# Scan and gated FFN on one core: the scan of chunks 1 to 5 as one unit of four batches, with B and C loaded as rows and turned on VectorE

## The chip, the core and the metric

The kernel runs on one core of a Trainium2 chip. A core has five engines with a queue each: TensorE (PE; its weight loads are shown as PEld), VectorE (DVE), ScalarE (ACT), GpSimd (POOL) and SyncE (SP), which here only issues DMAs. The metric is the device time of one execution in microseconds (us); of several runs the median is given.

## What is computed

A chunked state-space scan with 4 batches of 8 heads, 768 tokens, head size 32 and state size 16, and behind it a gated FFN over all 3072 tokens (model size 256, inner size 1536). Everything is float32.

```python
for c in range(nc):                                  # scan, per batch and head
    cum = np.cumsum(np.log(a)[chunk]); L = exp(cum[:, None] - cum[None, :]) * causal
    y_intra = ((C @ B.T) * L) @ x                    # within the chunk
    y_inter = (C @ state) * exp(cum)                 # from the state before
    state = exp(sum) * state + sum_j B_j x_j exp(cum[-1] - cum_j)
x = y.transpose(0, 2, 1, 3).reshape(B * S, H * D)    # then the FFN
out = (sigmoid(x @ w_gate) * (x @ w_val)) @ w_out
```

## The kernel before

**Chunks.** The 768 tokens are cut into six chunks of 128, each as two halves of 64. For each chunk the scan gives 4 x 128 = 512 rows of x, and the FFN runs over these 512 rows: twelve slices f of the inner size, each with a gate product `pg` and a value product `pv` (`products_of`, L784, six matmuls each, in which both operands are split into a high and a low part, `xh`/`xl` and `w`), then four output blocks `po` (`proj`, L821, L822, and L810 for chunk 0). I call the FFN over a chunk's rows its pass. In the pass of chunk 0 the first six slices take the weights whole (L775, the thin part), and the weights still arrive: each is clipped and split in five steps on VectorE, ScalarE and GpSimd (`split_w`, L323 to L336) and later cut into two parts (`part_w`, L351, L353).

**The scan before.** Chunk 0 has a class of its own (`FirstUnit`). For chunks 1 to 5 a unit is one chunk of one batch, and two batches share a step on TensorE. For each unit `products` turns B and C of 128 tokens on TensorE (`nc.tensor.transpose`, L393, L394, into the tile `pt`), and ScalarE copies and masks them (L404, L408, tile `bct`). For each pair there is then a product C times B (`multiply`, L473, 16 matmuls; I call it the multiply), on VectorE its weighing by the decays (`weigh`, L487), then on TensorE the product with x and with the decayed B (`within`, L499 and L506, 48 matmuls; 40 in the last chunk), on VectorE two masked local states (`chosen`, L514; L541), and on TensorE the part from the state before (L550, 16 matmuls; I call it the inter). ScalarE and VectorE cut the result into `xh` and `xl` (L564, L570). The decays come from a scan on VectorE of 128x512 for each unit (L428), whose rows `ab` are broadcast by DMA from a DRAM tile `a_z` that the kernel has written itself; the products of decays `pp` come in the same way from `a_p`.

**What sets the order.** `run()` is a planner in the kernel's own code: it takes the steps (`step(engine, cost, needs, makes)`) in the order of due times (the table `DUES` and rules such as `AHEAD`, `UNIT_T`, `STATE`) and of its own estimates, and writes one fixed instruction order for each engine. Each engine then runs its list in that order and waits at an instruction for what it needs. SP issues all loads and stores in one queue with eight lanes: a DMA waits until the DMA eight places before it is complete. PSUM gives three banks in turn (`ps_mm`) to `pg`, `pv` and `po`, so each such product needs the bank that was used three products before, and that is freed by ScalarE's sigmoid (for `pg`) or VectorE's multiplication (for `pv`, L735 in chunk 0, L739 later).

Of the kernel before, what the change touches and what calls it, by code (L numbers as in the profile page):

```python
# [8 lines left out]
F32 = mybir.dt.float32  # L9
# [37 lines left out]
GV0 = 1.75  # L47
# [22 lines left out]
def tile_ssd_then_gated_ffn(  # L70
# [25 lines left out]
    NDEC = 6  # L96
    NPRE = 5
# [163 lines left out]
    c4 = Cm.rearrange("b h s n -> s (b h) n")  # L261
    got = {}

    def pair_of(tag, c, b, shape):

        k = tag, c, b // 2
        if k not in got:
# [756 lines left out]
```

## Time and profile before

| what | value |
|---|---|
| three runs | 376.8, 377.87 and 378.27 us, median 377.87 us |
| the profiled execution | span 375.7 us from the first to the last instruction (no other time is given for it) |
| TensorE busy | 365.3 us, 97% |
| VectorE, ScalarE, GpSimd busy | 155.8, 151.2 and 153.9 us (41%, 40%, 41%) |
| first `pg` of chunk 0 | 24.70 us |
| first `pg` of chunk 1 | 98.03 us |
| first `pg` of chunk 5 | 322.68 us |
| end of the last `po` | 372.40 us |
| mean granted TensorE clock | 0.995 |

A busy share is an average over the whole span; what a change in one stage is worth is read from the timeline of that stage. The name left of an arrow in a row is what is written, the names right of it are read, x is the count. For float32 matmuls of the scan, and for L810, the trace has two records for each instruction. A bracket [0.67 <- ...] in a timeline row is idle time ahead of it and what ended it.

### The profile page before, as it was taken

How to read it: one execution, taken by the hardware profiler on the slowest of the kernel's cores; microseconds unless marked ns; L12 is line 12 of the kernel's file. 1: busy time of each engine (PE TensorE's matmuls, PEld its weight loads, DVE VectorE, ACT ScalarE, POOL GpSimd, SP SyncE). 2: the span in 40 equal slices, each digit the busy share in tenths (PEclk: the TensorE clock that was granted, in tenths of full speed). 3: DMA queues.
4: the chain of work that ended last, by engine and by line, in shares of the span. 5: the costliest groups of instructions: out<-in, count | busy, mean ns of one | idle time of the engine just before them, and what ended most of it. 6: DMA issues, size and time to landing. Idle time of an engine off the chain costs nothing.

```text
span 375.7 us, 8098 instructions
## 1 busy us (share of the span) xinstructions
PE 365.3 (97%) x3360; PEld 286.3 (76%) x3360; DVE 155.8 (41%) x280; ACT 151.2 (40%) x319; POOL 153.9 (41%) x161
## 2 busy tenths in 40 slices
PE   8879999989999999999999999999999999999996
PEld 2565478758788888887788888788877788888885
DVE  4774755854874234253431452550132440122201
ACT  2567578223536421436510435420335420244400
POOL 4346557573669540245430055430145420145410
PEclk9999999989999999999999999999999999999999
DMA  7998964087520043415502303120000000000000
GB/s 153 139 352 181 226 241 155 30 126 142 107 50 16 0 88 69 67 49 58 91 9 58 97 4 39 34 38 30 28 3 2 2 2 28 30 0 0 2 28 28
DMA packets 89270, 26.27 MB, mean 70 GB/s; under 512 B 76306, under 2 KB 82002, under 8 KB 89234
## 3 DMA queue, kind: packets, MB, share of 16 engines
q1 hardware_dynamic: 89234, 25.76, 30.7%
q8 instruction: 26, 0.43, 0.5%
q14 instruction: 10, 0.08, 0.1%
HBM read 22.41 MB, written 3.34 MB: 69 GB/s over the span
## 4 chain that ended last, share of the span: by engine, by line
PE 78%; SPq 12%; DMA 7%; issue 1%; DVE 1%; POOL 0%; DVEq 0%; POOLq 0%
PE pg L784 22%; PE pv L784 22%; PE po L821 15%; PE po L822 7%; SPq L275 4%; PE po L810 4%; DMA wr<-in_moe_w_gate_dram 3%; SPq L313 2%; PE pcb L499 2%; DMA a_z<-a 2%; SPq L309 2%; SPq L282 2%; SPq L288 2%; PE pcb L473 2%; DMA cn<-in_C_dram 2%; PE pcb L550 1%
## 5 line engine op out<-in xcount | busy, mean ns | idle before, releaser
L745 POOL TENSOR_TENSOR h<-g,h 128x512 fp32r<-128x512 f32 x60 | 79.0, 1316 | 124.6 <-ACT h L743 122.0
L784 PE MATMUL pg<-xh,w 128*128 128x512 f32 x264 | 93.8, 396 | 0.0
L784 PE MATMUL pv<-xh,w 128*128 128x512 f32 x264 | 93.7, 396 | 0.0
L821 PE MATMUL po<-w,h 128*128 128x512 f32 x228 | 81.8, 402 | 0.0
L739 DVE TENSOR_TENSOR g<-pv,g 128x512 f32<-128x512 f32 x60 | 41.4, 691 | 91.4 <-PE pv L784 86.6
L743 ACT CAST h<-g 128x512 fp32r<-128x512 f32 x60 | 37.3, 621 | 78.4 <-DVE g L739 78.4
L822 PE MATMUL po<-w,h 128*128 128x256 f32 x228 | 63.9, 280 | 0.0
L784 PEld LDWEIGHTS pg<-xh,w 128*128 128x128 f32 x264 | 49.5, 188 | 11.4 <-issue 0.5
L784 PEld LDWEIGHTS pv<-xh,w 128*128 128x128 f32 x264 | 49.6, 188 | 10.6 <-issue 0.2
L784 PE MATMUL pg<-xl,w 128*128 128x512 f32 x132 | 51.5, 390 | 0.0
L784 PE MATMUL pv<-xl,w 128*128 128x512 f32 x132 | 51.4, 390 | 0.0
L821 PEld LDWEIGHTS po<-w,h 128*128 128x128 f32 x228 | 42.8, 188 | 10.7 <-issue 0.2
L715 ACT ACTIVATE g<-pg 128x512 f32<-128x512 f32 x72 | 43.1, 599 | 19.4 <-PE pg L784 13.7
L822 PEld LDWEIGHTS po<-w,h 128*128 128x128 f32 x228 | 43.0, 189 | 0.2
L837 ACT COPY o<-po 128x256 f32<-128x256 f32 x20 | 7.5, 373 | 67.3 <-PE po L822 66.7
L839 DVE TENSOR_TENSOR o<-po,o 128x256 f32<-128x256 f32 x20 | 8.5, 425 | 59.8 <-ACT o L837 59.7
L353 POOL TENSOR_TENSOR w<-wr,w 128x512 fp32r<-128x512 f32 x18 | 24.7, 1371 | 14.2 <-ACT w L351 10.8
L428 DVE TENSOR_TENSOR_SCAN ab<-ab,delta 128x512 f32<-128x512 f32 x20 | 26.5, 1331 | 5.6 <-DMA ab<-a_z 5.6
L784 PEld LDWEIGHTS pv<-xl,w 128*128 128x128 f32 x132 | 24.8, 188 | 4.7
L784 PEld LDWEIGHTS pg<-xl,w 128*128 128x128 f32 x132 | 24.8, 188 | 4.6
L810 PE MATMUL po<-wr,h 128*128 128x256 f32 x96 | 24.9, 409 | 0.0
L336 POOL TENSOR_TENSOR wr<-wr 128x512 int32<-128x512 int32 x18 | 21.6, 1207 | 6.3 <-ACT wr L334 3.7
(106 smaller groups left out, 377.4 us busy)
## 6 DMA issues: line engine op xcount, KB each, us to landing
ab<-a_z SPq DMA_DIRECT2D x40, 128.0 KB
wr<-in_moe_w_gate_dram SPq DMA_DIRECT2D x6, 512.0 KB
wr<-in_moe_w_val_dram SPq DMA_DIRECT2D x6, 512.0 KB
wr<-in_moe_w_out_dram SPq DMA_DIRECT2D x6, 512.0 KB
out_dram<-o SPq DMA_DIRECT2D x24, 128.0 KB
xn<-in_x_dram SPq DMA_DIRECT2D x10, 256.0 KB
bn<-in_B_dram SPq DMA_DIRECT2D x10, 128.0 KB
cn<-in_C_dram SPq DMA_DIRECT2D x10, 128.0 KB
```

Source lines behind the costliest of these rows:

```text
L275: nc.sync.dma_start(t[:, b % 2 : b % 2 + n].rearrange("p b h n -> p (b h) n"), src[cs, b * H : (b + n) * H])
L336: nc.gpsimd.tensor_tensor(out=lw.bitcast(I32), in0=hw.bitcast(I32), in1=lw.bitcast(I32), op=ALU.add)
L353: engines[eng].tensor_tensor(out=lo, in0=lw, in1=hi.bitcast(F32), op=ALU.subtract)
L428: nc.vector.tensor_tensor_scan(out=t.rearrange("p h l -> p (h l)"), data0=t.rearrange("p h l -> p (h l)"), data1=delta.rearrange("p h l -> ...
L715: nc.scalar.activation(gs[k, f], pm, AF.Sigmoid)
L739: nc.vector.tensor_tensor(out=g, in0=pm, in1=g, op=ALU.mult)
L743: copies[eng](hh, g)
L745: engines[eng].tensor_tensor(out=hl, in0=g, in1=hh.bitcast(F32), op=ALU.subtract)
L784: nc.tensor.matmul(pm, w[:, part, kt, fs], xx[:, kt], start=(i == 0), stop=(i == 3 * NK - 1))
L810: nc.tensor.matmul(acc[:, :DM], hs[k, f][:, js], whole[NF + f // 2][:, f % 2], start=start, stop=stop, skip_group_check=True,)
L821: nc.tensor.matmul(acc, hh, w.rearrange("p i m -> p (i m)"), start=start, stop=False, skip_group_check=True)
L822: nc.tensor.matmul(acc[:, :DM], hl, w[:, 0, :], start=False, stop=stop, skip_group_check=True)
```

## The change

Chunk 0 keeps its units by batch. For chunks 1 to 5 the class `Scan` takes all four batches at once: one multiply of 32 matmuls (L505), four weighings in place (L509), one `within` of 96 matmuls (L520, L527; 80 in the last chunk), one `chosen` and one addition of 128x256, one inter of 32 matmuls (L469), one pair of `xh`, `xl` halves of 128x512.

B and C are no longer turned on TensorE. `load_rows` loads them in another arrangement (`bq`, `cq`): a partition is a head and one of 32 groups of four tokens, and holds 4 x 16 values in a row, 256 bytes. Each of B and C comes in eight loads per chunk, one for each batch and group of heads. VectorE then turns each batch by one transpose instruction in blocks of 32x32 (`turned`, L387), and ScalarE masks the turned C for all four batches in two instructions of 128x512 (`masked`, L400). B is still loaded a second time as tokens (`bn`) for the decayed B.

```diff
-            nc.tensor.transpose(pt[:, :L], bn, eye)
-            nc.tensor.transpose(pt[:, L : 2 * L], cn, eye)
-            yield step("act", 0.9 if c else 1.1, [], [("bct", u)], **{hold: -1})
+                for b in range(NB):
+                    nc.vector.transpose(
+                        t[:, b].rearrange("p (t f) -> p f t", f=NQ),
+                        got[tag, c][:, b].rearrange("p g (f n) -> p f g n", f=NQ),
+                    )
...
+        rows = src[:, :, c * L : (c + 1) * L].rearrange("b (q g) (t f) n -> b g q t (f n)", g=NG, f=NQ)
+        return [lambda b=b, g=g: nc.sync.dma_start(t[:, b, g], rows[b, g]) for b in range(NB) for g in range(NG)]
...
+            for b in range(NB):
+                multiply(pcb[:, :, b * L : (b + 1) * L], self.bt[:, b], self.cg[:, b])
+            for b in range(NB):
+                yield step("dve", 0.7, [("cb", c), ("scan", c, b), ("bdec", c)], [("mult", c)])
+                dec = got["ab", c]
+                weigh(dec[:, b], pcb[:, :, b * L : (b + 1) * L], dec[:, b])
```

Other loads are joined too: `ab` comes in two loads per chunk instead of eight, `bn` and `xn` in one each. Fading the state moves to GpSimd (`faded`, L426), as does the addition of the next state (L497). The table `DUES` is new, so the plan is new on every engine; one line of it before and after:

```diff
-    "result5_1": 271.1, "decays5_3": 170.5, "value4_1": 242.8, "value4_6": 193.7, "value4_7": 305.22, "value4_8": 307.96,
+    "p2_1": -0.1, "bq2_3": -64.1, "result0_0": 17.3,
```

TensorE, in the pass of chunk 4, where the scan of chunk 5 stands between the FFN's products. Before (`pt` are the turned B and C, `pcb20` the bank of the pair):

```order
L784 MATMUL pv4_6_3291<-xh4_2819,w7_569 128x512
L393 MATMUL pt5_3_3301<-eye_88,bn5_1_2678 128x128
L394 MATMUL pt5_3_3301<-eye_88,cn5_1_2680 128x128
L784 MATMUL pg4_7_3304<-xh4_2819,w6_553 128x512
L784 MATMUL pg4_7_3304<-xl4_2820,w6_553 128x512
L784 MATMUL pg4_7_3304<-xh4_2819,w6_553 128x512 x2
L784 MATMUL pg4_7_3304<-xl4_2820,w6_553 128x512
L784 MATMUL pg4_7_3304<-xh4_2819,w6_553 128x512
L499 MATMUL pcb20_3181<-m5_0_3208,xn5_0_2767 32x64 x16
L506 MATMUL pcb20_3181<-xn5_0_2767,bd5_0_2775 32x64 x4
L499 MATMUL pcb20_3181<-m5_1_3210,xn5_0_2767 32x64 x16
L506 MATMUL pcb20_3181<-xn5_0_2767,bd5_1_2779 32x64 x4
```

After, at the same pass (`bt`, `cg` are the turned B and the turned and masked C of all four batches):

```order
L793 MATMUL pv4_9_3117<-xh4_2705,w9_650 128x512
L520 MATMUL pcb5_3058<-ab5_2898,xn5_3006 32x64 x16
L527 MATMUL pcb5_3058<-xn5_3006,bd5_3091 32x64 x4
L520 MATMUL pcb5_3058<-ab5_2898,xn5_3006 32x64 x16
L527 MATMUL pcb5_3058<-xn5_3006,bd5_3091 32x64 x4
L520 MATMUL pcb5_3058<-ab5_2898,xn5_3006 32x64 x16
L527 MATMUL pcb5_3058<-xn5_3006,bd5_3091 32x64 x4
L520 MATMUL pcb5_3058<-ab5_2898,xn5_3006 32x64 x16
L527 MATMUL pcb5_3058<-xn5_3006,bd5_3091 32x64 x4
L793 MATMUL pg4_10_3214<-xh4_2705,w10_693 128x512
```

The four turns are gone, and three blocks stand where ten pieces stood: the multiply behind `pg8`, the `within` behind `pv9`, the inter behind `pv10`, with three and two products between them. (In the pass of chunk 1 the blocks stand behind `pg11` and among the first `po`.)

SP, loads for chunk 1 while chunk 0 is in its pass. Before:

```order
L313 DMA wr14_503<-in_moe_w_out_dram 128x2x512
L275 DMA bn1_0_523<-in_B_dram 128x16x16
L275 DMA cn1_0_525<-in_C_dram 128x16x16
L313 DMA wr16_540<-in_moe_w_out_dram 128x2x512
L309 DMA wr11_550<-in_moe_w_val_dram 128x2x512
L313 DMA wr13_560<-in_moe_w_out_dram 128x2x512
L313 DMA wr15_567<-in_moe_w_out_dram 128x2x512
L895 DMA a_z_109<-a0_113 32x12x64
L898 DMA a_p_110<-a1_114 32x768
L288 DMA ab2_0_701<-a_z_109 64x512 x2
```

After:

```order
L281 DMA cq1_377<-in_C_dram 128x1x64 x3
L275 DMA xn1_571<-in_x_dram 128x32x32
L293 DMA pp1_576<-a_p_110 128x1x128 x4
L305 DMA wr11_592<-in_moe_w_val_dram 128x2x512
L281 DMA bq1_331<-in_B_dram 128x1x64
L287 DMA ab1_600<-a_z_109 64x2048
L281 DMA cq1_377<-in_C_dram 128x1x64 x2
L309 DMA wr15_639<-in_moe_w_out_dram 128x2x512
L287 DMA ab1_600<-a_z_109 64x2048
L281 DMA cq1_377<-in_C_dram 128x1x64
```

`a_z` and `a_p` now go out ahead of two of the weights, and the last of the sixteen row loads of B and C is the last load ahead of the first stores.

VectorE, the same time, the end of chunk 0's pass. Before (`h0_8` frees the bank of `pv` of slice 8):

```order
L323 TENSOR_SCALAR wr15_567<-wr15_567 128x512
L735 TENSOR_TENSOR h0_8_755<-pv0_8_725,g0_8_732 128x512
L428 SCALAR_TENSOR_TENSOR ab2_0_701<-ab2_0_701,delta_99 128x512
L735 TENSOR_TENSOR h0_9_789<-pv0_9_765,g0_9_776 128x512
L330 TENSOR_SCALAR wr14_503<-wt14_757 128x512
```

After:

```order
L319 TENSOR_SCALAR wr15_639<-wr15_639 128x512
L387 STREAM_TRANSPOSE ct1_705<-cq1_377 128x4x32 x4
L744 TENSOR_TENSOR h0_8_711<-pv0_8_685,g0_8_682 128x512
L326 TENSOR_SCALAR wr13_468<-wt13_714 128x512
L408 SCALAR_TENSOR_TENSOR ab1_600<-ab1_600,delta_99 128x512
```

The four transposes of C stand ahead of `h0_8`, so the bank of `pv` of slice 8 comes free only behind the last row load of C.

## Rows read from the trace of the kernel before

**Rows 1.** The page's part on the engines: busy us, share of the span, instructions.

```profile
PE 365.3 (97%) x3360; PEld 286.3 (76%) x3360; DVE 155.8 (41%) x280; ACT 151.2 (40%) x319; POOL 153.9 (41%) x161
```

**Rows 2.** The waits of TensorE over the whole span: who waited for whom, us in total, times, longest.

```profile
PE pt L394 <- DMA cn<-in_C_dram: 2.4, 2, 1.7
...
PE pcb L506 <- POOL bd L438: 0.7, 1, 0.7
...
PE pt L393 <- DMA bn<-in_B_dram: 0.2, 1, 0.2
```

**Rows 3.** The timeline of TensorE, the pass of chunk 5, in which no scan is left: its first product, its first `po`, and its last block (start, length).

```profile
322.68 0.40 PE L784 MATMUL pg<-xh,w 128*128 128x512 f32 x1
...
355.34 0.39 PE L821 MATMUL po<-w,h 128*128 128x512 f32 x1
...
370.82 1.58 PE L829 MATMUL po<-w,h 128*128 128x256 f32 x12
```

**Rows 4.** The timeline of TensorE, pieces of the scan, each with what starts next: a multiply of 16 matmuls and one of 8 (chunk 0), a `within` of 48 and one of 40, the turns of one unit, an inter of 16.

```profile
156.49 0.69 PE L473 MATMUL pcb<-bct 32*64 32x128 f32 x32
157.12 0.50 PE L784 MATMUL pg<-xh,w 128*128 128x512 f32 x1
...
21.42 0.47 PE L473 MATMUL pcb<-bct 32*64 32x128 f32 x16
21.82 0.71 PE L197 MATMUL fill<-eye 128*128 128x128 f32 x4
...
169.59 0.46 PE L499 MATMUL pcb<-m,xn 64*32 64x64 f32 x32
...
170.71 0.33 PE L393 MATMUL pt<-eye,bn 128*128 128x128 f32 x1
...
288.59 0.45 PE L499 MATMUL pcb<-m,xn 64*32 64x64 f32 x32
...
289.59 0.50 PE L784 MATMUL pv<-xh,w 128*128 128x512 f32 x1
...
172.38 0.27 PE L393 MATMUL pt<-eye,bn 128*128 128x128 f32 x1
...
172.51 0.48 PE L784 MATMUL pg<-xh,w 128*128 128x512 f32 x1
...
173.98 0.39 PE L784 MATMUL pv<-xh,w 128*128 128x512 f32 x1
...
175.43 0.34 PE L550 MATMUL pcb<-cd,sn 32*64 32x64 f32 x8
175.60 0.29 PE L550 MATMUL pcb<-cd,sm 32*64 32x64 f32 x8
...
175.83 0.29 PE L550 MATMUL pcb<-cd,sm 32*64 32x64 f32 x8
176.06 0.50 PE L784 MATMUL pg<-xh,w 128*128 128x512 f32 x1
...
177.56 0.27 PE L393 MATMUL pt<-eye,bn 128*128 128x128 f32 x1
```

**Rows 5.** The timeline of TensorE from the first product of chunk 0 to the first of chunk 1: the thin part's first product, the first turn behind it, the first 16 `po` matmuls, the two waits, the slow `po`, the first product of chunk 1.

```profile
24.70 1.14 PE L764 MATMUL pg<-xw,wr 128*128 128x256 f32 x4
...
46.88 0.27 PE L393 MATMUL pt<-eye,bn 128*128 128x128 f32 x1
...
65.05 7.41 PE L810 MATMUL po<-wr,h 128*128 128x256 f32 x32
72.39 0.46 PE L499 MATMUL pcb<-m,xn 64*32 64x64 f32 x32
...
81.21 0.33 PE L394 MATMUL pt<-eye,cn 128*128 128x128 f32 x1 [1.67 <-DMA cn<-in_C_dram]
81.38 3.25 PE L810 MATMUL po<-wr,h 128*128 128x256 f32 x8
...
98.03 0.50 PE L784 MATMUL pg<-xh,w 128*128 128x512 f32 x1
```

**Rows 6.** The windows view, the us behind the longest wait: window, busy us of PE, PEld, DVE, ACT, POOL (with counts), granted clock, DMA share, GB/s.

```profile
82.00:83.00 1.00, 1.00 (x4) 0.82 (x3) 0.00 (x0) 1.00 (x4) 0.61 (x2) 0.50 1.27 214
```

**Rows 7.** The timeline of VectorE, four clips that waited for their weight: the weight with place 3 (its load is the 17th in SP's queue, counted from the first load), the one 23rd, the one 28th, and the one 36th.

```profile
20.84 0.57 DVE L323 TENSOR_SCALAR wr<-wr 128x512 f32<-128x512 f32 x1 [0.83 <-DMA wr<-in_moe_w_val_dram]
...
29.59 0.43 DVE L323 TENSOR_SCALAR wr<-wr 128x512 f32<-128x512 f32 x1 [1.04 <-DMA wr<-in_moe_w_gate_dram]
...
37.74 1.96 DVE L323 TENSOR_SCALAR wr<-wr 128x512 f32<-128x512 f32 x3 [0.20 <-DMA wr<-in_moe_w_val_dram]
...
50.49 1.00 DVE L323 TENSOR_SCALAR wr<-wr 128x512 f32<-128x512 f32 x1 [2.65 <-DMA wr<-in_moe_w_val_dram]
```

**Rows 8.** The groups by line and shape: busy us, mean ns of one, idle before. VectorE's multiplication and weighing of 128x512, its masking of 128x128, ScalarE's cast of 128x512.

```profile
L739 DVE TENSOR_TENSOR g<-pv,g 128x512 f32<-128x512 f32 x60 | 41.4, 691 | 91.4 <-PE pv L784 86.6 <-PE pt L393 4.8
L743 ACT CAST h<-g 128x512 fp32r<-128x512 f32 x60 | 37.3, 621 | 78.4 <-DVE g L739 78.4
...
L487 DVE TENSOR_TENSOR m<-pcb,ab 128x512 f32<-128x512 f32 x24 | 15.6, 683 | 8.8 <-PE pcb L473 8.8
...
L514 DVE TENSOR_TENSOR ml<-pcb,mask 128x128 f32<-128x128 f32 x10 | 2.9, 289 | 13.8 <-PE pcb L506 13.8
```

**Rows 9.** The timeline of SP's queue: the issue of three small loads of 64 KB.

```profile
58.46 1.90 SPq L296 DMA_DIRECT2D pp<-a_p  x3
```

More of the change, by code (lines that the diff above doesn't have):

```diff
@@ L464, in multiply @@
-    def multiply(pcb, at, *us):
-        for k, t in enumerate(us):
-            t.banks = pcb
-            t.pcb = pcb[:, :, (at + k) * L : (at + k + 1) * L]
-            for q in range(NQ):
-                qs = slice(32 * q, 32 * q + 32)
-                for i in range(2):
-                    half = slice(i * L2, (i + 1) * L2)
-                    nc.tensor.matmul(
-                        t.pcb[half, q], t.bct[qs, 0, half], t.bct[qs, 2:4, half], start=True, stop=True
-                    )
@@ new lines, in before, with faded, early @@
+            engines[eng].tensor_tensor(out=self.ct, in0=self.ct, in1=got["pp", c], op=ALU.mult)
+        def faded(self, state, i):
+            t = wk.tile([P, NB, NG * D], F32, tag="sp", name=f"sp{self.c}", bufs=1)
+            nc.gpsimd.tensor_tensor(
+                out=t, in0=state,
+                in1=got["pp", self.c][:, :, i * L2 + L2 - 1 : (i + 1) * L2].broadcast_to([P, NB, NG * D]), op=ALU.mult,
+            )
+            return t
+        def early(self):
+            c = self.c
+            yield step("pool", 0.7, [("S", c - 1)] + [("p", c, b) for b in range(NB)], [("sp", c)], port=True)
+            self.sp = self.faded(states[c - 1], 0)
@@ new lines, in state, with multiply @@
+        def state(self):
+            c = self.c
+            yield step("pool", 0.7, [("inter", c)], [], port=True)
+            sp = self.faded(self.s1, 1)
+            eng = yield step(("dve", "pool"), (0.42, 0.7), [("after", c)], [("S", c)], port=True)
+            states[c] = state_of(c, "sn", 2)
+            engines[eng].tensor_tensor(out=states[c], in0=sp, in1=self.after, op=ALU.add)
+    def multiply(out, bt, cg):
+        for q in range(NQ):
+            qs = slice(32 * q, 32 * q + 32)
+            for i in range(2):
+                half = slice(i * L2, (i + 1) * L2)
+                nc.tensor.matmul(out[half, q], bt[qs, half], cg[qs, :, half], start=True, stop=True)
@@ L495, in within @@
+    def within(m, xn, bd, out, local, first=True, more=True):
         for kt in range(NK):
@@ L656, in early, with state @@
             self.take(0)
+        def state(self):
+            b = self.b
+            yield step("dve", 0.24, [("after", 0, b), ("first", 0, b), ("p0",)], [("S0", b)] + [("S", 0)] * (b == NB - 1), port=True)
+            states[0] = state_of(0, "sn", 2)
+            nc.vector.scalar_tensor_tensor(
+                out=states[0][:, b], in0=self.s1, scalar=got["p0"][:, b, L2 - 1 : L2], in1=self.after, op0=ALU.mult, op1=ALU.add
+            )
     def first_products():
@@ L719, in value @@
         if (k, f) == (0, 0):
-            yield step("pe", GV0 / 2, [("whole", 1), ("pg half",), ("y", 3)], banks=1)
+            yield step("pe", GV0 / 2, [("whole", 1), ("pg half",), ("y", 0, 3)], banks=1)
             pm = first_half(1)
@@ new lines, in chunk, with first_unit @@
+    def chunk(due, c):
+        s = Scan(c)
+        for k, g in loads_of(c).items():
+            task(due - AHEAD, k, g)
+        task(due, f"turned{c}", s.turned())
+        task(due, f"masked{c}", s.masked())
+        task(due, f"before{c}", s.before())
+        task(due, f"decays{c}", s.decays())
+        task(due, f"early{c}", s.early())
+        task(due, f"scan{c}", s.scan())
+        if s.more:
+            task(due + STATE, f"state{c}", s.state())
+    def first_unit(due, b):
+        u = FirstUnit(b)
+        task(-9.0 + b, f"spread{b}", u.spread())
+        task(due, f"early0_{b}", u.early())
+        task(due, f"before0_{b}", u.before())
+        task(due - 30.0, f"products0_{b}", u.products())
+        task(due, f"decays0_{b}", u.decays())
+        task(due, f"result0_{b}", u.result())
+        task(due + STATE, f"state0_{b}", u.state())
@@ L979, in tile_ssd_then_gated_ffn @@
     for k in range(NCH):
-        for b in range(NB):
-            if k + 1 < NCH and k:
-                unit(t + UNIT_T + UNIT_D * b, k + 1, b)
+        if 0 < k < NCH - 1:
+            chunk(t + UNIT_T, k + 1)
         for f in range(NF):
```

444 lines of the change are left out of this document (198 added, 246 removed), and 24 rows, old and new, of the table DUES.

## Prediction

> **What bounds the kernel now.** The page's part on the engines comes first: TensorE is busy for 97% of the span, VectorE, ScalarE and GpSimd for 40 to 41% [rows 1]. So the sum is one of TensorE's own work and of its few waits, and the others count where they make it wait. The waits of TensorE are next: 2.4 us behind a load of C, 0.7 behind a decayed B, 0.2 behind a load of B [rows 2]; I found no other of weight. Then the timeline of TensorE gives the price of one product. The pass of chunk 5 holds no scan: 24 products from 322.68 to 355.34, so 32.66 / 24 = 1.361 us each, and four `po` to 370.82 + 1.58 = 372.40, so 17.06 [rows 3]. A pass without scan is 49.72 us. From the first product of chunk 1 at 98.03 [rows 5] to 372.40 lie five passes: 274.37 - 5 x 49.72 = 25.77 us are the scan of chunks 2 to 5, about 6.4 a chunk. Those pieces stand in TensorE's queue, not beside it, so a cheaper form of them shortens the span by as much.
>
> **Pieces of the scan, before.** The length of a piece is read from its start to the start of what follows, less what the break costs the product ahead of it [rows 4]. A multiply of 16 takes 157.12 - 156.49 = 0.63, one of 8 0.40, so 0.23 / 8 = 0.029 an instruction. A `within` of 48 takes 1.12, one of 40 1.00, so 0.0155 an instruction. An inter of 16 takes 0.63, and eight of its instructions 175.83 - 175.60 = 0.23, again 0.029. The turns of a unit take 0.13, and the product behind them 173.98 - 172.51 = 1.47 in place of 1.36: 0.24 together. The product ahead of an inter takes 175.43 - 173.98 = 1.45, the one behind it 177.56 - 176.06 = 1.50: each block costs 0.09 + 0.13 = 0.22 more than its own length. A chunk before is then 4 x 0.24 + 2 x (0.63 + 1.12 + 0.63 + 3 x 0.22) = 7.04; four are 28.2 less what is short in the last one and where two pieces touch, against 25.77 measured. I use the measured sum.
>
> **TensorE's pieces, after.** Of the edits this is the main one. The turns go. Multiply of 32: 0.63 + 16 x 0.029 = 1.09; `within` of 96: 1.12 + 48 x 0.0155 = 1.86; inter of 32: 0.63 + 16 x 0.029 = 1.09; three breaks: 0.66. A chunk is 4.70, the last one, with 80 in place of 96, 4.45. Chunks 2 to 5 cost 3 x 4.70 + 4.45 = 18.55. I add 0.7 for short waits at the blocks (below): 19.25, and the stretch from the first product of chunk 1 to the last `po` is 248.60 + 19.25 = 267.85 in place of 274.37: **6.5 us less**.
>
> **The start.** From the first product at 24.70 to 98.03 are 73.33 us [rows 5]. The thin part takes 22.18 (to 46.88), twelve products of the rest 16.32, and 48 `po` matmuls 3 x (72.39 - 65.05) = 22.02: 60.52 in all. The other 12.81 are the scan of chunk 1 (7.0), the waits (2.55: the 1.67 at 81.21, and the rest from [rows 2], of which I take all that is C or the decayed B), a slow stretch, and some 1.8 of breaks. The slow stretch is the clock: in 82 to 83 us, behind the longest wait, it was granted at 0.50, the level of 1.2 GHz [rows 6], after TensorE had stood idle for 1.67; eight records of `po` took 3.25 there [rows 5] where the rate of the first sixteen gives 4 x 0.459 = 1.84, so 1.4 lost. After, the scan costs 4.70, the breaks perhaps 0.5 beside its 0.66, and the turns, which waited for `cn`, are gone; without any wait the first product of chunk 1 would start at 24.70 + 60.52 + 4.70 = 89.9.
>
> It won't be without any wait, since the loads of chunk 1 now come in one lump. In SP's queue the clip of the 17th load ended its wait at 20.84 and that of the 23rd at 29.59: five weights lie between, 1.75 us each. The next stretch to 50.49 held five weights and six pieces of B, C and x of chunk 1: from 37.74 on, 12.75 - 5 x 1.75 = 4.0 for three pairs, 1.33 a pair [rows 7]. After, the last row load of C stands behind fourteen weights (24.5), `bn` and `xn` (2 x 2.7, two pairs each), two broadcasts `ab` taken as a weight each (3.5), `pp` and the stores (about 1), and sixteen row loads of 256-byte runs, half as many runs as `bn`; I take 0.1 each, 1.6: 20.84 + 36 = 56.8. Four transposes and two masks follow (4 x 0.29 + 2 x 0.62 [rows 8], and 0.9 of hops): the multiply could start near 60. Its place in TensorE's order, nine products behind the thin part, comes at 46.88 + 9 x 1.36 = 59.1. Behind the transposes VectorE has `h0_8` queued, which frees the bank that the gate product of slice 10 wants, so TensorE stands for about as long there. I take 1.5 in all: first product of chunk 1 at **91.4**, 6.6 us less. An idle time of that size was followed by the lower clock once [rows 5, 6]; this is in the range, not in the sum.
>
> **The other engines.** VectorE gets eight transposes a chunk. Its own masking of 128x128 takes 0.289, its 128x512 multiplication from PSUM 0.691 [rows 8]; a transpose reads and writes SBUF alone, 128x128, so I take 0.29, and the ends are 0.2 and 0.69. They replace nothing on VectorE, but that engine is at 41%. What counts is the chain before each block. Ahead of the multiply: one `h` or sigmoid's product (0.69), four C transposes (1.16), two masks on ScalarE (1.24) with a sigmoid between, beside three products of TensorE (4.08): short by 0.1 or so. Ahead of `within`: four weighings (4 x 0.683) and one 0.69, beside the three products between the blocks (4.08): it fits. Ahead of the inter: `chosen` and an addition of 128x256, less than 1.4 together, beside two products (2.72). So 0.7 in four chunks. GpSimd's fading of the state is off this path. The loads of later chunks have a whole pass of 54 us and cost nothing; if that cover failed, the row of C would show it as in [rows 2]. The Trainium skill, on the page "VectorE: DVE Perf Modes", section "The three transpose paths", gives 311 ns for a 128x128 bf16 transpose on VectorE (in 32x32 blocks only) and 390 on TensorE. By it the sum would move by less than 0.5 us; no row here has a VectorE transpose.
>
> **The sum.** The profiled execution has a span of 375.7, of which 3.3 lie behind 372.40. After: 91.4 + 267.85 + 3.3 = 362.5 us of span. The median of the three runs is 2.2 above the span before; the same after gives **364.7 us**, 3.5% faster.
>
> **Rivals.**
> *One unit waits as one.* With pairs, the other pair and its products lay between a step and its follower; with four batches in one chain each block waits for all four. For it: the three chains above fit TensorE's products to within some tenths, and a bank (`pv`) freed late stops TensorE as well. Against it: each of VectorE and ScalarE is idle over half of the time [rows 1]. Half a us at each of three blocks in four chunks is 6 us more: **370.7**.
>
> *Small loads are dear at the start.* Three small loads of 64 KB took 1.90 us to issue, 0.63 each [rows 9]. Sixteen of them at 0.63 are 10.1 in place of 1.6, and the last row of C comes at 65, the multiply 8.5 later than summed; the half clock behind such a wait would add to it. The gain at the start is used up, near **372.8**. Against it: SP's queue runs ahead of the transfers where weights fill them, and the row loads are spread between weights. The Trainium skill speaks for this rival: "DMA: Bandwidth & Descriptors" has the rule to batch transfers to 1 MiB or more, those under 64 KB being dominated by descriptors, and gives 0.95 us for 64 KB. By that price sixteen loads would be 15.2 us; the broadcasts of 64 KB here went out faster than that.
>
> *The transpose is dear on VectorE (the other side).* The operand is strided, four values apart, in blocks of 32. Each d above 0.29 adds 4 d to the chain ahead of each multiply, and 4 d less the slack of 0.6 ahead of the weighings, where B's turns crowd the same engine; over chunks 2 to 5 and the start (8 d) that is about 40 d less 2.4. At 0.69 [rows 8] this is 13.6 us and the gain is gone, 378.3; from there it is slower, and at 0.8 **382.7**. Against it: the nearest row in shape is 0.289.
>
> **Chances.** The forecast, 361 to 368: 0.63. One unit waits: 0.17. Small loads dear: 0.11. Transposes dear, slower: 0.07. The new plan does little though nothing of these shows: 0.02. The range leaves out the last three: its low end is the sum without the two waits (1.5 and 0.7) and 1.5 for a start of the first product that the new order of loads may move, 361.0; its high end takes in the first rival and a half clock behind it, 372.0. A measurement of this kernel can tell about 0.5%, 1.9 us, from no change. The second rival with more of the half clock behind it would reach no change or pass it (0.02 and 0.01 of its 0.11): faster 0.63 + 0.17 + 0.08 = 0.88, the same 0.02 + 0.02 = 0.04, slower 0.07 + 0.01 = 0.08.
>
> **What would show it.** In the profile after: `nc.tensor.transpose` of chunks 1 to 5 gone; the transposes on VectorE near 290 ns each (600 or more is the third rival); the first product of chunk 1 near 91 (98 is the second); the starts of passes 54 to 54.5 apart (56 is the first), 49.7 for chunk 5; blocks of 1.1, 1.9 and 1.1; among TensorE's waits one of 1 to 2 us at the end of chunk 0's pass and tenths at the blocks; the granted clock at 1.0 from 60 us on. I am wrong on TensorE if products between blocks no longer take 1.36, and wrong on the start if its first product moves from 24.7.

## The result and the profile after

The changed kernel takes 380.72 us (median of 4 runs, 380.42 to 381.37) against 377.62 before (4 runs): a ratio of 1.0092, with a 95% interval of 1.0068 to 1.0116. It is 0.9% slower where the prediction had it 3.5% faster. The profiled execution has a span of 379.2 us in place of 375.7, and of the 362.5 forecast: the sum missed by 16.7 us. Times and ratios are of runs in the faster of two states of the chip; the profiled execution of one experiment, turn_twice, fell into the slower one.

The page's engine part and its row on the queue that carries instructions, after (answers [rows 1]):

```profile
span 379.2 us, 7895 instructions
...
PE 357.1 (94%) x3320; PEld 283.4 (75%) x3320; DVE 153.5 (40%) x270; ACT 139.1 (37%) x259; POOL 153.6 (41%) x144
...
q8 instruction: 26, 0.43, 0.5%
```

TensorE works 8.2 us less than before, and the span is 3.5 us longer: what was saved, and more, went into waits. They stand in the list of TensorE's waits, after, where before had 2.4, 0.7 and 0.2 [rows 2] (who waited for whom: us in total, times, longest):

```profile
PE pg L793 <- DVE h L744: 6.8, 1, 6.8
PE pcb L520 <- issue: 1.6, 1, 1.6
PE pv L793 <- POOL w L349: 1.5, 1, 1.5
PE pcb L527 <- issue: 1.4, 1, 1.4
PE pg L793 <- issue: 1.3, 1, 1.3
```

One wait of 6.8 us is the largest. Three waits are for "issue", that is, for nothing that the profile shows, and before had none of that size.

The timeline of TensorE, after: the wait at slice 10, the multiply of chunk 1 and the products beside it, the first product of chunk 1, a stall inside the `within` of chunk 2, the three blocks of chunk 3, the last `po` (answers [rows 3 to 5]):

```profile
56.91 0.73 PE L793 MATMUL pv<-xh,w 128*128 128x512 f32 x2 [1.55 <-POOL w L349]
...
67.90 0.77 PE L793 MATMUL pg<-xh,w 128*128 128x512 f32 x1 [6.76 <-DVE h L744]
...
70.73 2.01 PE L505 MATMUL pcb<-cg,bt 32*64 32x128 f32 x64
72.67 0.80 PE L793 MATMUL pv<-xh,w 128*128 128x512 f32 x1
...
104.32 0.59 PE L793 MATMUL pg<-xh,w 128*128 128x512 f32 x1
...
145.18 0.25 PE L527 MATMUL pcb<-xn,bd 64*32 64x64 f32 x2 [1.42 <-issue]
...
184.62 1.21 PE L505 MATMUL pcb<-cg,bt 32*64 32x128 f32 x64
...
190.06 0.46 PE L520 MATMUL pcb<-ab,xn 64*32 64x64 f32 x32
...
195.06 0.34 PE L469 MATMUL pcb<-ct,sn 32*64 32x64 f32 x8
...
374.34 1.58 PE L838 MATMUL po<-w,h 128*128 128x256 f32 x12
```

The first product of chunk 1 is at 104.32, forecast at 91.4 and before at 98.03. From it to the end of the last `po` (374.34 + 1.58 = 375.92) are 271.60 us, forecast 267.85 and before 274.37. So the five passes did become shorter, by 2.8 in place of 6.5, and the start became longer by 6.3.

Why TensorE stood at slice 10 is read one engine on. VectorE, after, around it (answers [rows 7]):

```profile
63.83 0.43 DVE L319 TENSOR_SCALAR wr<-wr 128x512 f32<-128x512 f32 x1 [4.91 <-DMA wr<-in_moe_w_out_dram]
64.17 0.62 DVE L387 STREAM_TRANSPOSE ct<-cq 128x128 f32<-128x128 f32 x2
66.60 0.63 DVE L387 STREAM_TRANSPOSE ct<-cq 128x128 f32<-128x128 f32 x2 [1.81 <-DMA cq<-in_C_dram]
67.08 0.67 DVE L744 TENSOR_TENSOR h<-pv,g 128x512 f32<-128x512 f32 x1
```

VectorE waits 4.91 for weight 15 and 1.81 for the last row of C. `h0_8`, whose inputs had long been there, is queued behind both and frees the bank that TensorE wants; hence "DVE h" in the list. ScalarE stands behind the same row: its mask of the turned C is queued ahead of the sigmoid of slice 9 (L724), which frees the bank of `pg9`, and that sigmoid starts at 69.07. ScalarE, after:

```profile
67.27 0.72 ACT L400 ACTIVATE cg<-ct,of_g 128x512 f32<-128x512 f32 x1 [6.12 <-DVE ct L387]
```

Both loads come from one queue. SP's queue, after (start, time of the issues):

```profile
31.71 1.36 SPq L275 DMA_DIRECT2D bn<-in_B_dram  x1
33.11 8.28 SPq L281 DMA_DIRECT2D bq<-in_B_dram  x2
...
44.86 1.68 SPq L281 DMA_DIRECT2D cq<-in_C_dram  x3
...
47.15 4.67 SPq L293 DMA_DIRECT2D pp<-a_p  x4
51.87 0.46 SPq L305 DMA_DIRECT2D wr<-in_moe_w_val_dram  x1
...
54.74 0.48 SPq L309 DMA_DIRECT2D wr<-in_moe_w_out_dram  x1
...
55.80 0.56 SPq L281 DMA_DIRECT2D cq<-in_C_dram  x1
```

The queue is held for 8.28 us by two row loads, 7.70 of it by the first one behind `bn`. That is no price of a row load; before, a weight's load behind an `xn` held the queue as long:

```profile
21.05 8.25 SPq L309 DMA_DIRECT2D wr<-in_moe_w_gate_dram  x1
```

Then each row load takes 0.56 us to issue and carries 32 KB, a sixteenth of a weight, which takes 0.46 to issue. The windows view, after, shows what this does to the transfers, and what the wait does to the clock (answers [rows 6]; columns as there):

```profile
40.00:44.00 4.00, 4.00 (x10) 1.77 (x9) 1.60 (x3) 2.92 (x6) 3.40 (x4) 1.00 0.40 66
44.00:47.00 3.00, 3.00 (x8) 1.37 (x7) 1.96 (x5) 0.80 (x3) 1.47 (x2) 1.00 0.33 77
...
47.00:62.00 15.00, 12.57 (x51) 9.06 (x49) 6.31 (x13) 7.88 (x15) 6.57 (x7) 1.00 1.00 184
...
64.00:67.00 3.00, 0.00 (x0) 0.00 (x0) 1.19 (x5) 0.00 (x0) 0.00 (x0) 0.50 0.14 25
67.00:70.00 3.00, 2.10 (x5) 1.74 (x6) 2.53 (x6) 2.37 (x4) 1.32 (x1) 0.50 0.00 0
```

While row loads are issued the DMA engines are busy for a third of the time, at 77 GB/s, with two weights still to come that all wait for. About 4 x 0.60 + 3 x 0.67 = 4.4 us of transfer time go unused there, an estimate from these two rows. From 47 to 62 they are busy throughout (share 1.00), so weight 15, issued at 54.74, is there only at 63.8. And TensorE, idle from 61.1 to 67.9, was granted 0.50 in 64 to 70, the level of 1.2 GHz: `pg10` took 70.73 - 67.90 = 2.83 in place of 1.45, the multiply 1.94 in place of 1.14, `pv10` 2.01 in place of 1.49, together 2.70 lost.

The groups, after (answers [rows 8]; busy us, mean ns of one, idle before):

```profile
L387 DVE STREAM_TRANSPOSE ct<-cq 128x128 f32<-128x128 f32 x20 | 5.6, 390 | 1.8 <-DMA cq<-in_C_dram 1.8
L400 ACT ACTIVATE cg<-ct,of_g 128x512 f32<-128x512 f32 x10 | 7.2, 718 | 7.7 <-DVE ct L387 7.7
```

A single transpose takes 0.39 us, but the next one starts before it has ended: 20 of them keep VectorE busy for 5.6 us, 0.28 each. A group of four takes 1.10, where the prediction's chain had 4 x 0.29 = 1.16:

```profile
133.60 1.10 DVE L387 STREAM_TRANSPOSE ct<-cq 128x128 f32<-128x128 f32 x4
```

A mask takes 0.72, forecast 0.62.

### The profile page after: what moved, and what is told of

Its sections match the earlier page's. It is cut to its first block, busy times and chain, and to the rows that moved or that the text cites. A ratio compares the mean times of both kernels' runs of the same rounds, so it can differ in the third digit from the quotient of the medians.

```text
span 379.2 us, 7895 instructions
## 1 busy us (share of the span) xinstructions
PE 357.1 (94%) x3320; PEld 283.4 (75%) x3320; DVE 153.5 (40%) x270; ACT 139.1 (37%) x259; POOL 153.6 (41%) x144
## 4 chain that ended last, share of the span: by engine, by line
PE 78%; SPq 11%; DMA 5%; issue 3%; DVE 1%; ACT 0%; DVEq 0%; ACTq 0%
PE pg L793 22%; PE pv L793 22%; PE po L830 14%; PE po L831 7%; PE po L819 6%; SPq L281 4%; DMA cq<-in_C_dram 3%; DMA wr<-in_moe_w_gate_dram 3%; PE pcb L520 2%; PE pcb L505 2%; SPq L268 2%; SPq L271 2%; SPq L305 1%; PE pcb L469 1%; SPq L293 1%
## 5 line engine op out<-in xcount | busy, mean ns | idle before, releaser
L724 ACT ACTIVATE g<-pg 128x512 f32<-128x512 f32 x72 | 42.8, 595 | 26.2 <-PE pg L793 21.7
L349 POOL TENSOR_TENSOR w<-wr,w 128x512 fp32r<-128x512 f32 x18 | 23.9, 1332 | 21.6 <-ACT w L347 21.5
L408 DVE TENSOR_TENSOR_SCAN ab<-ab,delta 128x512 f32<-128x512 f32 x20 | 28.4, 1424 | 0.0
L332 POOL TENSOR_TENSOR wr<-wr 128x512 int32<-128x512 int32 x18 | 19.2, 1074 | 8.9 <-ACT wr L330 7.2
L819 PE MATMUL po<-wr,h 128*128 128x256 f32 x96 | 22.4, 390 | 0.0
```

What stands on the lines that cost most here:

```text
L332: nc.gpsimd.tensor_tensor(out=lw.bitcast(I32), in0=hw.bitcast(I32), in1=lw.bitcast(I32), op=ALU.add)
L349: engines[eng].tensor_tensor(out=lo, in0=lw, in1=hi.bitcast(F32), op=ALU.subtract)
L408: nc.vector.tensor_tensor_scan(out=t, data0=t, data1=delta.rearrange("p h l -> p (h l)"), initial=0.0, op0=ALU.mult, op1=ALU.add,)
L724: nc.scalar.activation(gs[k, f], pm, AF.Sigmoid)
L819: nc.tensor.matmul(acc[:, :DM], hs[k, f][:, js], whole[NF + f // 2][:, f % 2], start=start, stop=stop, skip_group_check=True,)
```

## The experiments

My theory after these rows: TensorE's own sum holds, and the miss is three waits. (a) VectorE stands behind two loads and holds `h0_8`, with the half clock behind that. (b) SP's queue issues small loads ahead of the last weights, so that weights 15 and 11 and `pp` come late. (c) TensorE stalls for its own instructions in the longer `within` blocks. Rivals: the transposes themselves are the price; longer blocks cost TensorE more than their count says; or the waits have one common cause, the amount of data. All edits are made on the changed kernel, so its 1.0092 is what each ratio is held against. Each ratio is to the kernel before as it ran beside that experiment. The table has the medians and the landmarks of the profiled executions, in us. A landmark is of one execution, which can lie some us off its median: queue_order's was the slowest of its eight, half_rows' the fastest of eight.

| kernel | median | ratio to before (95%) | first product of chunk 0 | of chunk 1 | end of last `po` |
|---|---|---|---|---|---|
| before | 377.62 | 1 | 24.70 | 98.03 | 372.40 |
| changed | 380.72 | 1.0092 [1.0068, 1.0116] | 24.27 | 104.32 | 375.92 |
| turn_late | 375.96 | 0.9987 [0.9957, 1.0017] | 26.33 | 99.30 | 370.93 |
| turn_late_w15 | 374.86 | 0.9926 [0.9899, 0.9953] | 24.33 | 97.30 | 370.71 |
| rows_first | 380.09 | 1.0063 [1.0034, 1.0092] | 26.38 | 101.81 | 374.89 |
| queue_order | 373.29 | 0.9898 [0.9870, 0.9925] | 26.99 | 99.41 | 370.94 |
| half_rows | 374.46 | 0.9927 [0.9895, 0.9959] | 27.22 | 95.35 | 367.31 |
| within_split | 379.42 | 1.0049 [1.0028, 1.0071] | 27.28 | 101.91 | 373.91 |
| page_shift | 380.87 | 1.0081 [1.0046, 1.0116] | 34.14 | 103.42 | 374.82 |
| pads | 376.99 | 0.9978 [0.9954, 1.0002] | 25.38 | 103.03 | 372.42 |
| turn_twice | 393.64 | 1.0416 [1.0356, 1.0476] | 27.70 | 106.43 | 394.18 |
| all_three | 377.33 | 0.9979 [0.9956, 1.0001] | 34.49 | 99.56 | 372.45 |
| queue_pool | 371.89 | 0.9837 [0.9795, 0.9880] | 27.08 | 96.13 | 367.29 |
| queue_pool_pads | 366.83 | 0.9705 [0.9687, 0.9724] | 25.89 | 92.48 | 361.96 |

**The transposes of C behind `h`.** In turn_late the C transposes of chunk 1 stand behind the last `h` of chunk 0, and its multiply behind the third `po` group:

```
# turned(), c == 1, C only
needs + [("h", 0, NF - 1)] + [(tag, c, i) for i in range(2 * NB)]
# scan(), c == 1: the multiply
needs = [("mult", 0, b) for b in range(NB)] + [("po", 3)]
# decays(), c == 1: [("ct", 1)] added
```

> The edit holds the four transposes of C for chunk 1, and the scans of its decays, behind h0_11 on VectorE, and chunk 1's multiply behind the third group of po of chunk 0; loads and their order are as in the changed kernel. Weight 15's clip still stands ahead of h0_8. Theory A (loads that come late in SP's one queue stop VectorE, and behind it the bank for slice 10): VectorE now waits at h0_8 for weight 15 alone, which in the changed kernel ended its wait at 63.83, so the 6.8 us wait of TensorE falls to about 3.5 to 4 and the time by 3 to 5 us, to 376 to 378. Theory B (chunk 1's scan is a chain too long for the place it has, whatever stands at h0_8): the wait goes to the multiply or the within, the first product of chunk 1 stays within 1 us of 104.3, and the time stays at 380 to 381.

Measured: the ratio falls by 1.05 points, and chunk 1 begins 5.0 us earlier. VectorE, turn_late:

```profile
63.48 0.83 DVE L325 TENSOR_SCALAR wr<-wr 128x512 f32<-128x512 f32 x1 [4.74 <-DMA wr<-in_moe_w_out_dram]
64.23 1.28 DVE L751 TENSOR_TENSOR h<-pv,g 128x512 f32<-128x512 f32 x2
```

The clip of weight 15, still ahead of `h0_8`, waits as it did (4.74 and 4.91), yet TensorE waits only 1.9 for `h` (forecast 3.5 to 4) and no half clock follows. `h0_8` comes at 64.23 in place of 67.08, and `pg10` doesn't wait for it: it starts at 61.52, as soon as ScalarE, which no longer stands behind a mask, has done the sigmoid of slice 9, so here it seems to take the bank of `pg9` and not, as the rule of banks in turn has it, that of `pv8`. So what stood behind the last C row, on both engines, made the wait long for TensorE. turn_late_w15 moves that clip behind `h0_9` as well:

```
# split_w(), first step
[("raw", i)] + [("h", 0, 9)] * (i == 15)
```

> As turn_late, and weight 15's clip is held behind h0_9. Theory A: no load is left ahead of h0_8, the 6.8 us wait is gone, and with it most of the half clock behind it (2 to 3 us); first product of chunk 1 at 94 to 97, time 371 to 374. Theory B: waits of the same sum at the multiply, the within or the first po of chunk 0; time 379 to 381.

The wait for `h` is gone and 0.6 points more are gained (374.86 us, just above the forecast's 374). Two waits of 3.0 in sum for weights on GpSimd's side stay (1.5 in the changed kernel, 0.8 in turn_late): holding VectorE back brings no weight sooner.

**The order of SP's queue.** rows_first takes the row loads of chunk 1 out earlier, so that all of B and C lies there in time:

```
-"cq1_4": 237.8, "cq1_0": 76.9, "cq1_7": 54.5, "bq1_7": 18.5
+"cq1_4": -40.0, "cq1_0": -40.0, "cq1_7": -40.0, "bq1_7": -40.0
# transposes of c == 1 behind h0_6 (B) and h0_7 (C); scans of c == 1 behind h0_11
```

> Three late row loads of C and one of B go ahead of the second x, the decays and weights 11 and 15 in SP's queue; the transposes keep their places ahead of h0_7 and h0_8 on VectorE, the scans of the decays go behind h0_11; the plan puts weight 15's clip behind h0_9 by itself. Theory A: the last row of C lands 10 us or more earlier, nothing stops h0_8, first product of chunk 1 at 94 to 98, time 371 to 375. If the row loads are late by their own issue (some 0.55 us each in one queue) wherever they stand, h0_8 still waits for 3 us or more, and the time is above 377.

Its ratio is 1.0063, no gain that stands out from the changed kernel's; the forecast of 371 to 375 us missed (380.09). TensorE's waits, rows_first:

```profile
PE pv L794 <- ACT w L347: 2.1, 1, 2.1
PE pg L794 <- ACT xh L481: 2.0, 1, 2.0
```

The wait at slice 10 is gone. A late weight 11 took its place, and a late `xh` of chunk 1, the result of its scan: the planner, which this edit let reorder TensorE too, had put the `within` behind all 48 `po` matmuls of chunk 0 instead of behind the first 24. So this run doesn't test the loads alone. It does show that a load moved ahead in a full queue pushes another back. queue_order turns it round, with the plan otherwise as it was: the two last weights go ahead of the row loads, and x and both `ab` behind the rows (SP's order from `bn` on):

```
-bn1, bq1 x2, a_z, bq1 x2, a_p, bq1 x2, cq1 x3, xn1, pp1 x4, wr11, bq1, ab1, cq1 x2, wr15, ab1, cq1
+bn1, bq1 x2, a_z, wr11, wr15, bq1 x2, a_p, bq1 x2, cq1 x3, pp1 x4, bq1, cq1 x3, xn1, ab1 x2
```

> Only SP's queue is in another order, every other engine's list is the changed kernel's: weights 11 and 15 go behind the store of a_z, where the trace shows the transfer engines near idle (41 to 47 us), and the last row loads of B and C and the products of decays go ahead of the second x and the decays. Theory A (the place of these loads in SP's queue made the 6.8 us wait, the half clock behind it and half of the other waits): the wait at slice 10 falls below 1.5 us, first product of chunk 1 at 94 to 98, time 371 to 374. Theory B (chunk 1's scan is too long a chain for the end of chunk 0's pass): the wait goes to the multiply, the within or the first product of chunk 1, which stays above 102; time 379 to 381.

Measured: 0.9898 (373.29 us, in the forecast's 371 to 374), 1.9 points under the changed kernel and faster than before, with chunk 1 begun 4.9 us earlier (at 99.41, forecast 94 to 98). The wait for `h` falls from 6.8 to 1.3. The bytes are the same, so their amount is not the cause. The low share of the DMA engines goes where the rows now are, with no weight left behind them; the windows view, queue_order:

```profile
50.00:53.00 3.00, 3.00 (x15) 2.46 (x14) 2.22 (x4) 1.90 (x4) 1.15 (x1) 1.00 0.33 80
```

half_rows leaves out half of the row loads of chunk 1:

```
# load_rows(): for b in range(NB if c > 1 else 2); transposes of c == 1 read b % 2
```

> Eight of the sixteen row loads of chunk 1 are left out, those of batches 2 and 3 of B and C; the transposes of these batches read the rows of batches 0 and 1 in their place, so the output of chunk 1 is another. All lists are else the changed kernel's. If a row load costs the queue its issue time (some 0.55 us each while the transfer engines idle), eight less bring what stands behind 4 us or more earlier: the wait at slice 10 falls from 6.8 to 2 to 3.5 us, time 375 to 377.5. If the rows cost only their bytes (256 KB less, under 1 us) and the lateness is that of the weights, x and decays ahead of them, the wait stays above 5.5 us and the time at 379.5 to 381.

SP's queue and VectorE, half_rows:

```profile
50.09 0.58 SPq L306 DMA_DIRECT2D cq<-in_C_dram  x1
50.72 0.47 SPq L334 DMA_DIRECT2D wr<-in_moe_w_out_dram  x1
```

```profile
58.58 1.27 DVE L344 TENSOR_SCALAR wr<-wr 128x512 f32<-128x512 f32 x1 [1.33 <-DMA wr<-in_moe_w_out_dram]
...
59.77 1.10 DVE L412 STREAM_TRANSPOSE ct<-cq 128x128 f32<-128x128 f32 x4
```

Seven of the eight loads left out stood ahead of weight 15, whose load goes out at 50.72 in place of 54.74: 4.02 / 7 = 0.57 us each, what one takes to issue. All eight are a quarter of a MB, half a weight, whose transfer at 1.75 a weight [rows 7] would take 0.9 us; so they don't cost by their bytes at a weight's rate. Whether it is the loads that count or their 256-byte runs isn't parted, since half_rows halves both. The wait at slice 10 shrinks to 0.5 (forecast 2 to 3.5), and chunk 1 begins 9 us earlier in this execution; the median is 6 us lower than the changed kernel's (374.46, forecast 375 to 377.5). So (a) and (b) are two forms of one thing, the order and number of SP's loads.

**The stalls for "issue".** within_split parts the `within` of 96 into two of 48 with two products between:

```
 # scan(), before the third batch of within
+if b == 2: yield step("pe", 0.95, [("all", done["all"] + 2)], [("y", c)])
```

> The within block of each chunk is cut into two of two batches each, with two products (or two po groups) between. Theory F (TensorE's instructions come in 16 KB pieces, and a block of 192 matmul records in 1.9 us uses one up faster than the next comes): the three stalls of 1.3 to 1.6 us that the trace puts down to issue are gone, against five more breaks of 0.22: 3 us less, 377 to 378.5. Rival G (they are waits on another engine that the profile doesn't show): stalls of the same size stay somewhere in the two halves, and the time is 380.5 to 382.

The stalls over 0.3 us are all gone, but the five passes take 373.91 - 101.91 = 272.00 us against 271.60, and the median, 379.42, lies between the two forecasts. An added break a chunk (0.22 by [rows 4]) and the inter, which now stands one product behind `within` and finds VectorE not done (in chunks 3 to 5 it takes 1.72, 1.52 and 1.61 in place of 1.09), ate most of the gain. So the stall belongs to the long dense block, but shorter blocks are no cure. The windows view of the changed kernel shows the stall of chunk 2 with what stood ahead of it:

```profile
142.50:142.60 0.10, 0.10 (x28) 0.10 (x17) 0.00 (x0) 0.00 (x0) 0.00 (x0) 1.00 0.81 164
143.80:145.10 1.30, 0.00 (x0) 0.00 (x0) 0.00 (x0) 0.00 (x0) 0.00 (x0) 1.00 0.00 0
```

At 142.5, where no load of data is under way, a packet of 16 KB moves; 1.2 us later TensorE stops, at full clock, and all other engines rest. The page counts 26 such packets on the queue for instructions, and 3320 / 26 = 128 matmul records, with as many of weight loads, a packet. All three stalls begin 0.7 to 1.2 us after the start of such a packet and end 2.3 to 2.6 us after it. Products, six records in 1.36 us, take 29 us for 128; a `within` of 96 takes 2.04: only in the blocks can TensorE reach the end of a packet before the next is there. If that is so, the place of a block in the count of records decides. Let its place be the number of matmul records ahead of it, modulo 128. In the runs up to here the uncut blocks that stalled stand at 56, 72 and 48 (chunks 1, 2 and 5), those that did not at 80 and 0 (chunks 3 and 4) and 104 (chunk 1 of rows_first). The expectations count the same places from the block to the end of a piece: 72, 56, 80 and 48, 0, 24. pads shifts them by issuing some multiplies again, 24 matmuls (48 records) in chunk 1 and 16 (32 records) in chunk 4:

```
-for b in range(NB): multiply(...)
+for b in [0, 1, 2][: {1: 3, 4: 2}.get(c, 0)] + list(range(NB)): multiply(...)
```

> The instruction stream is shifted without touching the start: in chunk 1 the multiplies of three batches are issued twice (24 matmuls, 48 records more), in chunk 4 those of two batches (16 matmuls, 32 records more); all lists are else the changed kernel's. The within blocks then stand at 24, 8, 0, 48 and 0 records behind the end of an instruction piece, places at which no block stalled so far. Theory F: no issue stall over 0.5 us behind 60 us; 4.3 us less, 1.2 us more for the 40 matmuls: 376.5 to 378.5. Rival G: three stalls of the same size, 381 to 382.5.

TensorE's waits, pads:

```profile
PE pg L818 <- DVE h L769: 7.0, 1, 7.0
...
PE pcb L494 <- issue: 0.3, 1, 0.3
```

More work, and 1.1 points less time (376.99 us, forecast 376.5 to 378.5): the stalls are gone, the wait at slice 10 stays as it was. The stretch from the first product of chunk 1 is 269.39 in place of 271.60. page_shift, which came ahead of pads, tried the same with twenty small multiplies at the very front:

```
+for i in range(20):
+    nc.tensor.matmul(warm[:, :8], warm_sb, warm_sb[:, :8], start=True, stop=True)
```

> Twenty matmuls of eight columns (forty records) are added behind the three warming ones at the start, so that every later block stands forty records further in TensorE's instructions; nothing else is changed. Theory F (instructions come in pieces of 128 matmul records; with the within blocks at 72, 56 and 80 records from the end of a piece TensorE stalled, at 48, 24 and 0 in these runs it did not): the blocks now stand at 32, 16, 8, -40 and 40, none stalls, TensorE has no issue stall over 0.5 us behind 60 us, and the time is 3 to 4.5 us less, 376 to 378. Rival G (the stalls are bound to what these blocks wait for on other engines): the same three stalls, time 380.5 to 381.5.

The windows view and a wait, page_shift:

```profile
16.00:24.00 8.00, 8.00 (x97) 3.61 (x95) 4.98 (x7) 3.23 (x9) 2.06 (x4) 0.50 0.99 313
```

```profile
PE pcb L522 <- issue: 2.2, 1, 2.2
```

The forecast of no stall and 376 to 378 us missed: three stalls became one, of 2.2 in chunk 4, whose block now stands at 40, a place that no run had tried. And with the twenty multiplies ahead the clock was granted at 0.50 in 16 to 24 us, and the first product of chunk 0 came 9.9 us later. That they are the cause of the clock isn't shown: nine of the other twelve executions also had a stretch at 0.50 in their first 30 us, though a shorter one (at most 10.2 us, against 17.1 here and 20.5 in all_three). The thin part ends 8.4 us later too (the first product behind it is at 55.90, in the changed kernel at 47.53). The delay is made up behind it, where the wait for `h` is 2.6 in place of 6.8 and two shorter waits are gone; the ratio is 1.0081, the same as the changed kernel's.

The traces of all kernels say more on these stalls than their blocks' places do. Waits of TensorE for "issue" of over 0.5 us behind 60 us come 25 times in ten of the fourteen profiled executions, 0.84 to 2.17 us long. They are four different points of the program, 140 to 170 records from the starts of the blocks of chunks 1, 2, 5 and, in page_shift and all_three, 4. Yet the matmul record at which TensorE stops has 81 to 85 for its place at all four, and each stall ends 2.3 to 2.7 us after the start of the 16 KB packet before it. Waits on other engines would have no reason to share a place in the count of records. A stall can also cost more than its length: those of 1.8 us in queue_order, 1.9 in queue_pool and 2.2 in all_three were followed by 3.4 us at a granted clock of 0.50, that of 1.9 in turn_late was not.

**The transposes themselves.** turn_twice issues each transpose of chunks 2 to 5 a second time, 32 more:

```
-nc.vector.transpose(t[:, b]..., got[tag, c][:, b]...)
+for _ in range(2 if c > 1 else 1): nc.vector.transpose(t[:, b]..., got[tag, c][:, b]...)
```

> Each transpose of chunks 2 to 5 is issued twice on VectorE, all else is the changed kernel's: 4 x 0.39 = 1.55 us more ahead of C's masks, as much for B. By the prediction's rival of dear transposes, whose cover is 0 ahead of the multiply and 0.6 ahead of the weighing, each of the four multiplies waits 1.2 to 1.6 us more: 385 to 387. If VectorE has cover there, the time stays within 1 us of 380.7.

VectorE and TensorE's waits, turn_twice:

```profile
136.38 2.85 DVE L412 STREAM_TRANSPOSE ct<-cq 128x128 f32<-128x128 f32 x8
```

```profile
PE pcb L530 <- ACT cg L425: 9.3, 4, 3.0
```

The median is 393.64 us, 12 to 13 above the changed kernel's and well above both forecasts. A group of eight takes 2.85 where one of four took 1.10: 1.75 us more for VectorE, 14 in the eight groups of four chunks. So nearly each us that was put into this chain came out as time. The forecast had B's groups ahead of the weighing alone; they stand ahead of the multiply too, since it reads both. The landmarks are of the slowest of the four runs (399.43 us), so the 287.75 us from chunk 1 on are no measure of the price. In that execution the multiply waits 9.3 in four chunks, where the changed kernel has one wait of 0.6 there, and the lower clock follows those waits. So the chain ahead of the multiply has next to no slack beyond the real price, though VectorE is busy for 40%; but at 1.10 a group it still fits, and the transposes are not where the 16.7 us went.

**Together.** all_three joins queue_order, page_shift and GpSimd's fading step `sp1` set behind the low part of weight 11:

> The order of queue_order, the twenty matmuls of page_shift, and GpSimd's fading of the state for chunk 1 (which waits for the products of decays) moved behind the low part of weight 11, so that no weight's part waits behind it. If the three causes are apart and each is as read: queue 7 to 9 us, stalls 3 to 4.3, GpSimd 1 to 1.5 less than the changed kernel, 366 to 370, 2 to 3% faster than before. If they cover one another, 371 to 375.

0.9979 (377.33 us), above both forecasts: chunk 1 begins where it does in queue_order (99.56 and 99.41), and one stall, of 2.2, is left with the half clock behind it. With the first product of chunk 0 at 34.49 the front is late, and I read it so that weights which come earlier hide less of that; this wasn't parted. queue_pool leaves the twenty multiplies out, and mends what queue_order still waits for: `pp`, for which GpSimd stood 4.00 ahead of the low part of a weight, and `ab`, for which VectorE stood 3.94 ahead of `h0_9`. VectorE, queue_order:

```profile
66.92 1.66 DVE L433 TENSOR_TENSOR_SCAN ab<-ab,delta 128x512 f32<-128x512 f32 x1 [3.94 <-DMA ab<-a_z]
```

```
# queue_order, and: sp1 on GpSimd behind w11's low part;
# the first two scans of chunk 1's decays behind h0_11 on VectorE
```

> The order of queue_order, GpSimd's fading of chunk 1's state behind the low part of weight 11, and the first two scans of chunk 1's decays behind h0_11 on VectorE, since in queue_order VectorE waited 3.9 us for the decays there. If these were all that TensorE still waited for at the end of chunk 0's pass, the two waits of 1.3 us of queue_order go: first product of chunk 1 at 24 + 71 to 72 after its first product of chunk 0 at 24, time 369.5 to 372. If the scans are now late for the within, a wait of 2 us or more stands there and the time is 372 to 374.

0.9837 (371.89 us, forecast 369.5 to 372), and its list of waits has stalls for "issue" at its head (1.9, 1.4, 1.1). queue_pool_pads adds the shift of pads:

> queue_pool and pads together. If stalls and waits are apart: 3 us less than queue_pool, 366.5 to 369, 2.3 to 3% faster than before. If the blocks that stall cover something else, as much as queue_pool.

366.83 us (366.18 to 366.96; forecast 366.5 to 369), ratio 0.9705 [0.9687, 0.9724]: 3% faster than before, and faster than both kernels. TensorE's waits, queue_pool_pads:

```profile
PE pg L809 <- DVE mr L560: 1.1, 1, 1.1
...
PE pcb L494 <- issue: 0.2, 1, 0.2
```

With the waits gone, the first product of chunk 1 stands 92.48 - 25.89 = 66.59 us behind that of chunk 0 (forecast 91.4 - 24.70 = 66.7), and the five passes take 269.48 (forecast 267.85). With the loads and the stalls out of the way, both sums of the prediction nearly hold.

## Why the prediction was wrong

- **TensorE's pieces: right, the `within` 0.18 short.** Multiply 1.14 and inter 1.09 (forecast 1.09 each), `within` 2.04 (1.86), the product ahead of a block 1.45 and behind it 1.49. The one pass with a scan and neither stall nor wait, chunk 3's, takes 54.6 (forecast 54 to 54.5). The blocks themselves put 4 x 0.23 = 0.9 us on the sum.
- **"I take 1.5 in all" at the end of chunk 0's pass: wrong, and the step that failed most.** It was 6.76. Under it lies "I take 0.1 each" for the row loads. They take 0.56 each to issue, and half_rows gives 0.57. I had the rival with 0.63 in hand, from three issues of 64 KB [rows 9], and took a sixth of it on the argument that SP runs ahead of the transfers. It does not where the transfers are small: a third of DMA time is used there. The Trainium skill has the rule, in "DMA: Bandwidth & Descriptors", section "Bandwidth", that transfers under 64 KB are dominated by descriptors; the low share here goes with it in direction. Its 0.95 us for 64 KB is the time of a transfer, so the prediction's 15.2 us of queue and the issues here don't measure the same thing. The rival had the last row of C nearly right (65, measured 66.6). Its 372.8 counted only that row; it left out that the same queue holds weights 15 and 11 and `pp`, and that ScalarE's sigmoid waits behind the same row as VectorE's `h0_8`.
- **The half clock behind that wait: named, priced at nothing in the sum.** It took 2.70 us. Wait and clock are 5.26 + 2.70 = 7.96 of the start's miss of 80.05 - 66.7 = 13.35. The rest: 1.55 for the low part of weight 9 on GpSimd, whose queue stood behind `pp`; 1.62 of stall; 1.08 in the thin part for `mr`; 1.1 that I can't place.
- **The five passes: 3.75 over the forecast.** 2.70 are two stalls (1.42 + 1.28), a wait on no list of mine: before, `within` had 48 matmuls and no stall over the tenths showed. A wait of 0.61 at chunk 2's multiply lies within the 0.7 I had given to blocks, and I place the other 1.05 on the longer `within` (0.9).
- **The sum of the miss:** 13.35 + 3.75, less 0.43 by which the first product of chunk 0 came earlier, is 16.7.
- **"One unit waits as one": did not come.** In five passes one block wait over 0.3 us shows.
- **"The transpose is dear": did not come.** One takes 0.39, but what the chain pays is 1.10 for four, under the 1.16 that was forecast. turn_twice shows that the rival's slope was real: 12 to 13 us for 14 us more of VectorE's time.
- **The gain at the start was lost on one small number, chosen at the low end of its bounds.** At 0.63 a load my own row led to 372.8. With 2.70 for the clock that I named beside it and 4.32 for three stalls that I did not know of, that is 379.8, past no change; the queue's order alone (queue_order) brings the gain back to 1%.

## What to carry to other kernels

Price a small DMA by what its issue takes on its queue, and then ask which large load stands behind it and who waits for that: here sixteen loads of 32 KB held back two weights, and their order alone was worth 1.9%. Take what an instruction costs in a chain from a group of them (1.10 for four transposes), not from the length of one (0.39), since one can start before the last has ended. An engine that is idle for half of the time still blocks when a waiting instruction stands ahead of one that frees a bank; move what waits behind what releases. When short matmuls are joined into long blocks, look for stalls without a releaser and compare them with the instruction queue's packets and with their place in the count of records.

## What the hardware showed that I had not expected

TensorE seems to outrun its instructions: three stalls of 1.3 to 1.6 us followed a 16 KB packet on the instruction queue by about a us, inside or right behind blocks of 96 small matmuls (80 in the last chunk), and 40 matmuls more (pads) took them away. The Trainium skill, "Runtime: NRT & Kernel Launch", section "Instruction fetch mechanics", has the refill in 16 KiB blocks, as here, and calls the fetch hidden; these stalls say that it is not always. That the shift in place removes the stalls is shown, and that they keep to one place in 128 records; that the fetch is their cause rests on this place and on the packets' times, and what triggers a refill stays open. Some executions showed the clock at half around 20 to 28 us; this wasn't tried.
